# The last 512 tokens of a fused attention and MLP kernel, scored by four head groups of 128 tokens in place of one head group of 512

## The chip, the cores and the metric

The kernel runs on one core of one Trainium2 chip. The metric is the device time of one execution in microseconds (us); the median of three runs is given, and one more execution was profiled. A core has five engines that run side by side and wait for each other by semaphores: PE (TensorE: matrix products; PEld is its weight load), DVE (VectorE), ACT (ScalarE: activation functions such as exp), POOL (GpSimd) and SP (SyncE, which here issues the DMAs).

## What is computed

A transformer block with parallel branches over 2048 tokens of width 512: one layer norm, multi-query attention (32 heads of 16, one shared K and V), and an MLP of width 1792 with gelu.

```python
xn = _layernorm(x)                                  # (1, 2048, 512)
q = (xn @ wq).reshape(B, S, 32, 16)...              # 32 heads of 16
k, v = xn @ wk, xn @ wv                             # one K and V for all heads
p = softmax(einsum("bhqd,bkd->bhqk", q, k) * 0.25)  # no mask
attn = einsum("bhqk,bkd->bhqd", p, v)... @ wo
h = gelu(einsum("bsd,df->bsf", xn, w1) + b1)        # F = 1792
out = x + attn + einsum("bsf,fd->bsd", h, w2) + b2
```

All inputs and the output are bf16.

## The kernel before, in words

**Tiles.** The tokens are cut into 4 blocks of 512 (`TBW`; `NTB` = 4), the heads into 8 groups of 4 (`NGR`, `HG`), the keys into 16 tiles of 128. A score tile is 128 keys x 512 columns: one head of a group against the 512 tokens of a block. 4 blocks x 8 groups x 16 key tiles x 4 heads are 2048 tiles (`NTILE`), and a block and group pair, `gg` from 0 to 31, is a run of 64 of them (`TPG`). Three tiles make a unit; there are 683 units, numbered by `u`.

**Scores** (`scores`, L962). A unit's three scores are one trio on PE, in 32-row tiling, into half of the six score banks of PSUM; the two halves alternate. The weights are K, the moving operand is `QT[32 rows, g, :]`, 512 columns of group g.

**Exponentials.** Each tile takes one of two ways, as the table `DTAB` says with one letter per unit. Most go through ACT (`exp`, L983, the instruction at L999), two or three tiles per instruction, and then take one product with V. The others go through DVE: an affine step to int16 bits (`p1`, L1030), then in batches (`close_batch`) integer steps that make three more buffers (L1077) and a last step per tile (L1073), which POOL takes when it fits; each buffer and its shifted version are a weighted summand of the exponential, so such a tile needs five products with V (`pv_mm`, L1043).

**Product with V.** The products run in 32-column tiling: four of them, one per head of the group, stand side by side in PE and add into one bank, `pO`. V has a column of ones in row 16 of each head, so the denominators come with the sum.

**Normalization** (`o_evac`, L1087). When the 64 tiles of a group are through, DVE copies `pO` to `Of` (L1089). DMAs bring the denominators into `den` and the four heads' rows into `OfP`; for every second group DVE takes the reciprocals, they go to DRAM and come back spread over rows as `rbP`, and two multiplications of 128x256 (L1120, POOL or DVE) write `oTp` for the pair. Group 30 is normalized alone, with a half filled pair whose other rows carry b2 (`wopE`, L1112). The last group, 31, has a way of its own (`o_norm_last`): DVE copies (L1127), PE spreads the denominators with `selB` (L668), ACT takes the logarithm and exp(-ln) (L1134, L1137), and DVE multiplies (L1140).

**Side work.** Everything else PE does in the loop also runs in 32-column tiling through one bank, 7 (`mm4`, L674, four matmuls of 128*32 by 512, one set): Q for the next block (`q_pack`, and `q_m`, which writes an extra row per head into QT), the MLP's first product (`h_mm`), and the output tiles of 128 tokens x 512: the MLP's second product (`y_mm`, 14 sets), the attention's output product (`wo_mm`, 4 sets) and b2. Gelus run on ACT in two blocks, after units 182 and 512.

**The end.** In blocks 0 to 2 an output tile is closed by one DVE addition (`out_tile`, L1246) and a store. In block 3 a head group covers all 512 tokens, so no tile can be closed before the last group. `y_tile` (L1251) puts what it can into bank 7, with the first two of the four pairs (`FIN_G` = 2), and DVE sets three tiles aside in f32 (L1256); the fourth stays in bank 7. After the loop the last pairs' products go into the score banks 2, 3, 4 and bank 7, the last group's product (`wol`, 4 sets, one per tile) follows, DVE adds three tiles (L1362), ACT copies the fourth (L1365), and four stores follow.

**What sets the order.** A planner in the program (`Prog.schedule`, L230) lists all instructions with costs in us and picks for each engine the next one, simulating the engines with constants; the order it finds is fixed and written out per engine, with semaphore waits (`emit`). For PE it holds that each of the four column groups is busy for 0.216 per product, that four follow each other by 0.006, that the next round starts when all four are free, and that a change between score trios (rows) and the rest (columns) costs `SWITCH` = 0.1. Side work becomes due at units given by the tables `HP` (h_mm), `YP` (output tiles), `YF`, `QK` and `Q3` (Q). The chip doesn't see these numbers; only the order that comes out of them.

Of the kernel before, what the change touches and what calls it, by code (L numbers as in the profile page):

```python
# [10 lines left out]
P = 128  # L11
# [10 lines left out]
SWITCH = 0.1  # L22
WIN = 3.413
# [28 lines left out]
FIN_G = 2  # L52
FIN_F = 0
# [3 lines left out]
TBL = 1  # L57
DMASK = {".": (), "0": (0,), "2": (2,), "a": (0, 1), "b": (1, 2), "x": (0, 1, 2),
         "o": (0,), "t": (2,), "A": (0, 1), "B": (1, 2), "X": (0, 1, 2)}
CLOSE = "otABX"  # L60
DTAB = "ooo0tt.020t.0t.00o000.o0.0tt0..oo2222o.02.t02t02..o2o.22ot202.0.0oo.200t22.o0o22o0.0020.22t0.t.2o.t.o2ttto.00o2oo0..o2000o0ot.t.002o0002tt.200.o0to.o.t2otott0.t.2.0o000oo...000o2000toxXxB2to222t0020t.0t.oo202t.t.00t2o202ot02.0t0t.02.2oot2.o0t.00o2200220.o.2oo022.tot.ot02o002.2.t0tt02t2t...000ot..o222tt22t..202o.22.o0..002o.2o2tt0t.2t0.020t0..22t2o..02o2020t22.t0002t22o..o00t2.t.o2o20o2t02.0t2.0t.00t.2t2ott2ot0t2to.22.oto2..o200tt2t.0t002ot00..0too22o20tt2...02.ott.2t0.0ott..00t0.00oto..tt2t0202tot0t.0220toaBXXBto2o02.t202o0.02t.22ooo2t.2002o0.o00.o2ot.t202ooto.00o222t0..to200t0oo.2.0o.2t00o20o2t22.0t.tt0t2o2.0t.oo00t00o2.o.o02ot2.t.2ttt200oot.202o0.0t..totoo0.t2o2o.2.t2to..."
# [14 lines left out]
HP = ((87.13167,22,66.82083,147.91108,40.38849,110.84753,55.66665,14,50.53259,112,20.66845,152.08006,61.80125,39.6289),(150.38812,79.48637,93.96663,107.61124,166.80472,0,0,0,0,0,0,0,0,0),(291.76004,310.12719,295.27265,322.59733,262,325.24506,298.5666,286,298,435.55883,304,280,433.01683,498.53492),(475.57156,486,469.88268,498,442,0,0,0,0,0,0,0,0,0))  # L76
YP = ((201.09452,184.17265,220,250),(346.3059,388.90013,354.32695,420.90269),(522.38115,516.36879,560.84805,588.7863),(613.17749,604.45936,628.95944,659.10039))
# [37 lines left out]
class Prog:  # L115
# [84 lines left out]
    def pick_pe(self, t, cand, allr, mode, visit, cgbusy):  # L200
# [3 lines left out]
        if mode == "col":  # L204
            end = max(cgbusy)
            if t < end - 0.01:
                if t < end - 0.216 + 0.03:
# [22 lines left out]
    def schedule(self):  # L230
# [31 lines left out]
        opened = None  # L262
        aend = 0.0
# [9 lines left out]
        while left:  # L273
# [13 lines left out]
            if e == "pe":  # L287
                op = self.pick_pe(t, cand, ready["pe"], mode, visit, cgbusy)
                st = max([free["pe"]] + cgbusy) if mode == "col" else max([free["pe"], pend + SWITCH] + cgbusy)
# [97 lines left out]
            if e == "pe":  # L387
# [3 lines left out]
                if op.kind in ("pv", "side"):  # L391
                    cg = op.tag[1]
                    st = max(t, cgbusy[cg], free["pe"])
                    if mode != "col":
                        st = max([t, pend + SWITCH] + [c + SWITCH for c in cgbusy])
                    op.start = st
                    cgbusy[cg] = st + 0.216 * slow
# [15 lines left out]
                elif op.kind != "side":  # L413
                    m = {"S": "row", "side": "col"}.get(op.kind, "full")
                    w = SWITCH if m != mode else 0.0
# [13 lines left out]
            if e == "pe":  # L429
# [5 lines left out]
                pend = op.start + op.occ * slow  # L435
# [31 lines left out]
    def settle(self):  # L467
        free = {e: 0.0 for e, _ in self.SECTIONS}
        mode, cg, pend, aend = None, [0.0] * 4, 0.0, 0.0
        for op in self.ops:  # L470
# [3 lines left out]
            if op.eng == "pe":  # L474
                if op.kind in ("pv", "side") or (op.kind == "fill" and occ > 0.15):
                    t = max(t, cg[op.tag[1]]) if mode == "col" else max([t, pend + SWITCH] + [c + SWITCH for c in cg])
                    cg[op.tag[1]] = t + 0.216
                    mode, end = "col", t + 0.006
                else:
                    m = "row" if op.kind == "S" else "full"  # L480
                    w = SWITCH if m != mode else 0.0
                    t = max([t, pend + w] + [c + w for c in cg])
                    mode, end = m, t + occ
                pend = t + occ
# [8 lines left out]
    def emit(self):  # L493
# [4 lines left out]
        for op in self.ops:  # L498
# [40 lines left out]
def bass_parallel_sum__grouped_kv_mqa__dense_activation_gelu__prompt_kernel(  # L539
# [33 lines left out]
    with ExitStack() as es:  # L573
# [16 lines left out]
        wol = sb([P, D], bf, "wol")  # L590
# [14 lines left out]
        wopE = sb([P, D], bf, "wopE")  # L605
# [33 lines left out]
        oT = sb([P, TBW], bf, "oT")  # L639

# [287 lines left out]
        setup(lambda e: e.memset(wol[:], 0.0), w=["wol"], occ=0.4, due=24.0, after=late)  # L928
        setup(lambda e: e.tensor_copy(selB[:].rearrange("p (j r) -> p j r", j=4), ident[:, 16:113:32].unsqueeze(2).to_broadcast([P, 4, 32])),
              r=["ident"], w=["selB"], occ=0.3, due=24.0, after=late)  # L930
        setup(lambda e: e.memset(wopE[:], 0.0), w=["wopE"], occ=0.4, due=24.0, after=late)
        dma("sp", wop[:], A_wo.rearrange("(g p) n -> p g n", p=P), "d_wo", w=["wop"], after=late)
        dma("sp", wopE[0:64, :], A_wo[(H - 2 * HG) * Dh:(H - HG) * Dh, :], "d_we", w=["wopE"])
        dma("sp", wopE[64:65, :], B_b2.rearrange("(o n) -> o n", o=1), "d_we", w=["wopE"])
        for j in range(HG):
            dma("sp", wol[32 * j:32 * j + Dh, :], A_wo[(H - HG + j) * Dh:(H - HG + j + 1) * Dh, :], "d_wl", w=["wol"])
# [5 lines left out]
        TPG = HG * NT  # L942
        NTILE = NTB * NGR * TPG
# [17 lines left out]

        def scores(u):  # L962
# [3 lines left out]
            for i, t in enumerate(ts):  # L966
                gg, kt, j = tile_of(t)
                tb, g = divmod(gg, NGR)
# [3 lines left out]
                r += [k for k in q_rows(g) if k not in r]  # L972
# [113 lines left out]

        def o_evac(gg):  # L1087
            i = gg % 2
# [4 lines left out]
            end = gg == NTB * NGR - 2  # L1093
# [5 lines left out]
            if h or end:  # L1099
# [11 lines left out]
            if end:  # L1111
                dve(lambda e: e.memset(oTp[64:P, sl, :], 1.0), r=[("Of", i)], w=[("oTp", sl)], n=200, lock=True)  # L1112
            if h or end:
                n = 64 if end else P
# [107 lines left out]
        def wo_mm(tb, i, ps, start=False, bk=7, al=1.5, stop=False):  # L1222
            for n, p in enumerate(ps):
                pp = tb * NGR // 2 + p
                hs = [h for h in range(2) if 2 * pp + h < NTB * NGR - 1]
                assert all(2 * pp + h in onorm for h in hs) and 2 * (pp + NPR) + 1 not in onorm
# [184 lines left out]
```

## Time and profile before

| What | Value |
|---|---|
| median of three runs | 745.96 us (745.7 to 746.35) |
| the profiled execution, its own time | 746.57 us |
| its span in the profile | 744.8 us |
| exponentials on ACT (L999) | 678 instructions, 676.3 us |
| first step of DVE tiles (L1030) | 554 instructions, 375.0 us |
| matmuls of scores (L976) | 2048, mean 385 ns |
| last steps of DVE tiles: POOL, DVE (L1073) | 453 and 115 |

The span runs from the first to the last instruction of the profiled execution. Busy times of an engine are the union of its instructions' times; instructions overlap a little, so a mean duration is longer than the distance from one start to the next. An idle time is followed by what ended it.

### The profile page before, as it was taken

Reading aid. Unit: us, or ns where it says so; the run is one execution under the profiler, and the core shown is the slowest. Engines: PE = TensorE matmul, PEld = TensorE weight load, DVE = VectorE, ACT = ScalarE, POOL = GpSimd, SP = SyncE. Lnnn points to the kernel's source line nnn. Section 1 sums busy time; section 2 is a strip of 40 time slices with the busy share of each in tenths; the row PEclk is TensorE's granted clock in tenths of the full one; section 3 lists DMA queues with packets and bytes.
Section 4 is the critical chain, followed back from the end, with each engine's and each line's share of the span. In section 5 each row is a group of like instructions: output and inputs, shape, how many; then the busy total and the mean of one; then the engine's idle time right before and its main releaser. Section 6 shows DMA issues by size and latency. Waiting matters only on the chain.

```text
span 744.8 us, 22104 instructions
## 1 busy us (share of the span) xinstructions
PE 731.4 (98%) x9128; PEld 226.7 (30%) x9130; DVE 731.0 (98%) x1401; ACT 728.9 (98%) x759; POOL 389.3 (52%) x539
## 2 busy tenths in 40 slices
PE   7999999999999999999999999999999999999998
PEld 5332222222233222223222322223233323222223
DVE  7899999999999999999999999999999999999996
ACT  8899999999999999999999999999999999999996
POOL 5554565646314656553544655555634665556452
PEclk9999999999999999999999999999999999999999
DMA  9200100100010010100101110110001001010011
GB/s 310 70 16 20 31 9 16 26 8 18 12 36 18 14 46 24 24 24 11 36 5 30 32 31 22 22 27 14 23 14 28 20 16 45 16 39 17 13 39 33
DMA packets 32159, 23.41 MB, mean 31 GB/s; under 512 B 16386, under 2 KB 27580, under 8 KB 32060
## 3 DMA queue, kind: packets, MB, share of 16 engines
q1 hardware_dynamic: 31004, 21.97, 11.1%
q8 instruction: 73, 1.20, 0.7%
q14 instruction: 26, 0.21, 0.1%
q10 hardware_dynamic: 1056, 0.03, 0.1%
HBM read 13.15 MB, written 2.35 MB: 21 GB/s over the span
## 4 chain that ended last, share of the span: by engine, by line
ACT 65%; PE 30%; DVE 3%; DMA 1%; issue 0%; SPq 0%; POOL 0%
ACT E L999 64%; PE pAll L1043 13%; PE pAll L976 9%; PE pAll L674 7%; DVE Dt L1030 1%; DVE Dt L1077 1%; DMA x_sb<-in_A_x_dram 1%; PE pAll L668 0%; PE pAll L814 0%; DVE stats L763 0%; ACT xnT L819 0%; PE pAll L1372 0%; ACT ub L796 0%; DVE Dt L1073 0%; DVE QT L865 0%
## 5 line engine op out<-in xcount | busy, mean ns | idle before, releaser
L999 ACT ACTIVATE E<-pAll 128x1024 bf16<-128x1024 f32 (+1 forms) x678 | 676.3, 1212 | 3.0 <-PE pAll L976 2.7
L1073 POOL TENSOR_SCALAR Dt<-Dt 128x512 int16<-128x512 int16 x453 | 348.5, 769 | 318.8 <-DVE Dt L1077 143.6
L1043 PE MATMUL pAll<-Dt,V 128*32 128x512 bf16 x2840 | 414.3, 383 | 0.8 <-DVE Of L1089 0.8
L1030 DVE TENSOR_SCALAR Dt<-pAll 128x512 int16<-128x512 f32 (+1 forms) x554 | 375.0, 694 | 1.2 <-PE pAll L976 0.6
L1077 DVE TENSOR_SCALAR Dt<-Dt 128x1024 int16<-128x1024 int16 (+5 forms) x524 | 292.6, 582 | 0.3
L1043 PE MATMUL pAll<-E,V 128*32 128x512 bf16 x1480 | 278.4, 384 | 0.0
L976 PE MATMUL pAll<-QT,KT 32*128 32x512 bf16 x2048 | 267.4, 385 | 3.6 <-ACT E L999 1.4
L976 PEld LDWEIGHTS pAll<-QT,KT 32*128 32x128 bf16 x2048 | 66.8, 91 | 282.2 <-ACT E L999 265.2
L1043 PEld LDWEIGHTS pAll<-Dt,V 128*32 128x32 bf16 x2840 | 108.0, 95 | 110.5 <-issue 70.4
L674 PE MATMUL pAll<-xnT,w_sb 128*32 128x512 bf16 x896 | 104.7, 382 | 0.0
L1043 PEld LDWEIGHTS pAll<-E,V 128*32 128x32 bf16 x1480 | 66.3, 94 | 49.7 <-issue 36.0
L674 PE MATMUL pAll<-w_sb,x_sb 128*32 128x512 bf16 x448 | 71.7, 383 | 0.0
L674 PE MATMUL pAll<-w_sb,ub 128*32 128x512 bf16 x448 | 70.1, 383 | 0.0
L674 PE MATMUL pAll<-wop,oTp 128*32 128x512 bf16 x240 | 45.3, 383 | 0.0
L674 PEld LDWEIGHTS pAll<-xnT,w_sb 128*32 128x32 bf16 x896 | 29.8, 95 | 19.8 <-issue 8.8
L1073 DVE TENSOR_SCALAR Dt<-Dt 128x512 int16<-128x512 int16 x115 | 30.1, 281 | 0.0
L1120 POOL TENSOR_TENSOR oTp<-OfP,rbP 128x256 bf16<-128x256 f32 x29 | 23.2, 808 | 11.7 <-DVE Dt L1030 5.1
L674 PE MATMUL pAll<-xnT,wq_sb 128*32 128x512 bf16 x256 | 23.4, 383 | 0.0
L1089 DVE COPY Of<-pAll 128x512 f32<-128x512 f32 x31 | 21.0, 679 | 0.0
L1176 DVE TENSOR_SCALAR ub<-pAll,b1T 128x512 bf16<-128x512 f32 x28 | 20.8, 742 | 0.2 <-PE pAll L1043 0.2
L674 PEld LDWEIGHTS pAll<-w_sb,x_sb 128*32 128x32 bf16 x448 | 17.6, 95 | 8.1 <-issue 6.6
L674 PEld LDWEIGHTS pAll<-w_sb,ub 128*32 128x32 bf16 x448 | 17.6, 94 | 6.9 <-issue 5.7
(125 smaller groups left out, 256.4 us busy)
## 6 DMA issues: line engine op xcount, KB each, us to landing
OfP<-Of SPq DMA_DIRECT2D x124, 32.0 KB, 2.0
rbP<-rden_rows SPq DMA_DIRECT2D x124, 32.0 KB, 1.8
w_sb<-in_B_w_dram SPq DMA_DIRECT2D x2, 1792.0 KB, 13.4
x_sb<-in_A_x_dram SPq DMA_DIRECT2D x8, 256.0 KB, 4.6
x_sb<-in_A_x_dram SPq DMA_DIRECT2D x16, 128.0 KB, 2.3
QT<-qp SPq DMA_DIRECT2D x124, 16.0 KB, 1.8
out_dram<-x_sb SPq DMA_DIRECT2D x12, 128.0 KB, 1.8
wq_sb<-in_A_wq_dram SPq DMA_DIRECT2D x1, 512.0 KB, 6.5
```

Of the source, the lines that this page charges most:

```text
L674: add("pe", lambda e, c=c, j=j: e.matmul(o[c, :], l[:, c], rh, start=start, stop=stop, tile_position=(0, 32 * j)), r, [(k, j) for k in w] ...
L976: ins = e.matmul(o, l, rh, start=True, stop=True, tile_position=(q0, 0))
L999: o = act(lambda e: e.activation(E[:, s0:s0 + na, :], bank(b0, na).rearrange("p (a n) -> p a n", a=na), ACT.Exp, scale=LN2 / 128.0), w=[B( ...
L1030: op = dve(lambda e: e.tensor_scalar(Dt[:, s:s + n, :], bank(bk, n).rearrange("p (a n) -> p a n", a=n), float(127 * 128) + SPL_D, SPL_MIN, ...
L1043: add("pe", lambda e, a, b: e.matmul(pO[32 * j:32 * j + 32, :], V1[:, v, kt, :], rhs, start=a, stop=b, tile_position=(0, 32 * j)), r=r + [ ...
L1073: add("pool", lambda e, d=d, k=k: e.tensor_scalar(d, d, 1.0, float(k), ALU.mult, ALU.add), [], [(("D", base[o > 0] + q), o)], occ=PL_OCC, ...
L1077: dve(lambda e, d=view(o, nb), q=view(i, nb), k=k: e.tensor_scalar(d, q, float(k), None, ALU.add), r=keys(i), w=keys(o), n=nb * n * TBW, m ...
L1089: dve(lambda e: e.tensor_copy(Of[:, i, :], pO), w=["O", ("Of", i)], allow=0.0)
L1120: "pool", lambda e, c=c: e.tensor_tensor(oTp[0:n, sl, c], OfP[0:n, s, c], rbP[0:n, s, c], ALU.mult),
L1176: dve(lambda e: e.tensor_scalar(ubs[tb % 2][:, ft, :], pM, b1T[:, ft:ft + 1], None, ALU.add), r=["b1T"], w=M4 + [ukey(tb, ft)], n=TBW + 57 ...
```

## The change

In the last block a `gg` no longer stands for one group against 512 tokens but for four groups (0 to 3, then 4 to 7) against 128 tokens. The 64 tiles of a `gg` are still 16 key tiles x 4 heads, and a tile still has 512 columns, now 4 groups x 128 tokens. After each second `gg` 128 tokens have all their heads. So:

- `o_quarter` takes the place of `o_evac` for `gg` 24 to 30. It normalizes each `gg` by itself: one reciprocal, 8 DMAs into `OfP`, 8 into `rbP`, one multiplication of 128x256 into `oTq`, which lies in a part of `xnT` that is no longer needed.
- The first three output tiles of the block are closed by `out_tile` like those of the blocks ahead. The fourth (`y_last`) waits in bank 7 with the MLP, x and two of its four pairs; after the loop come four sets with the last `gg` (one per group, weights `wol`), one ACT copy and one store.
- `wol` is loaded at unit 300 into another part of `xnT` (`w_last`, 9 DMAs), with b2 in it; the memsets and loads of the old `wol` and `wopE` at the start go.
- The planner's constants change: 0.216 becomes `C_OCC` = 0.197 for the time that a column group is held, with 0.0105 more in the first round of a visit; 0.1 becomes 0.115 and 0.1055 for the changes to rows and to columns.
- The tables `DTAB`, `HP` and `YP` are others, from a search. `Q3`, `QK` and the gelu places stay.
- In `emit` a wait may name a later value of a semaphore that another wait of the same instruction implies already.

```diff
+SW_ROW = 0.115
+SW_COL = 0.1055
+C_OCC = 0.197
+C_FIRST = 0.0105
...
-YP = (...,(613.17749,604.45936,628.95944,659.10039))
+YP = (...,(593.39845,625,654.09462,657.83105))
...
-                        st = max([t, pend + SWITCH] + [c + SWITCH for c in cgbusy])
+                        st = r1 = max([t, pend + SW_COL] + [c + SW_COL for c in cgbusy])
                     op.start = st
-                    cgbusy[cg] = st + 0.216 * slow
+                    cgbusy[cg] = st + (C_OCC + (C_FIRST if st < r1 + 0.1 else 0.0)) * slow
...
-                t = max(t, best.pop(s, 0))
+                t = max(t, best.pop(s, 0), kn[s])
...
+        wol = xnT[:, :, TBW:2 * TBW]
+        oTq = xnT[:, :, 2 * TBW:3 * TBW]
...
+        def groups(gg):
+            if gg < G3:
+                return slice(gg % NGR, gg % NGR + 1), slice(0, TBW)
+            c = gg - G3
+            return slice(HG * (c % 2), HG * (c % 2) + HG), slice(P * (c // 2), P * (c // 2) + P)
...
-                pieces.append((bank(3 * x + i), KT[q0:q0 + 32, kt * P:(kt + 1) * P], QT[q0:q0 + 32, g, :], q0))
+                pieces.append((bank(3 * x + i).rearrange("p (a n) -> p a n", a=n), KT[q0:q0 + 32, kt * P:(kt + 1) * P],
+                               QT[q0:q0 + 32, gs, cs], q0))
...
+        def o_quarter(gg):
+            i = s = gg % 2
+            q, k = divmod(gg - G3, 2)
+            dve(lambda e: e.tensor_copy(Of[:, i, :], pO), w=["O", ("Of", i)], allow=0.0)
...
+            for h in range(2):
+                for j in range(HG):
+                    r0 = 64 * h + Dh * j
+                    dma("sp", OfP[r0:r0 + Dh, s, 0:2 * P].rearrange("p (a n) -> p a n", a=2),
+                        Of[32 * j:32 * j + Dh, i, :].rearrange("p (a h n) -> p h a n", a=2, h=2)[:, h], f"d_of{s}{h}",
+                        r=[("Of", i)], w=[("OfP", s, h, j)])
+            dve(lambda e: e.reciprocal(den[:, s, 0:1, :], den[:, s, 0:1, :]), r=[("den", s, 0)], w=[("den", s, 0)], n=136)
...
+            o = add("pool", lambda e: e.tensor_tensor(oTq[:, 2 * k:2 * k + 2, P * q:P * q + P], v3(OfP), v3(rbP), ALU.mult),
+                    keys, [("oTq", k, q)] + (tr(8, 12) if q == 0 else []), occ=ON_OCC, lat=PL_LAT, allow=PL_DUE, kind="pl", lock=True,
+                    docc=vcost(TBW // 2))
...
+        at(300, w_last)
...
-                    at(YP[tb][i], lambda tb=tb, i=i: y_tile(tb, i), 0.6)
-                at(YF, lambda tb=tb: wo_mm(tb, 3, range(FIN_G, NGR // 2), al=WF_ALLOW))
+                    at(YP[tb][i], lambda tb=tb, i=i: (out_tile if i < 3 else y_last)(tb, i), 0.6)
+                at(YF, lambda tb=tb: wo_mm(tb, 3, range(2), al=WF_ALLOW))
...
-        FB = (2, 3, 4, 7)
-        for i in range(3):
-            wo_mm(tb, i, range(FIN_G, NGR // 2), start=True, bk=FB[i], al=WF_ALLOW)
-        for i in range(4):
-            mm4(bank(FB[i]), oT[:, i * P:(i + 1) * P], wol[:, :], False, True,
-               r=[("oTl", i // 2), "wol"], w=[B(FB[i])], due=0.0)
...
+        for g in range(4):
+            mm4(pM, oT[:, g * P:(g + 1) * P], wol[:, g, :], False, g == 3, r=[("oTl", g // 2)] + WOL,
+                w=[B(7)], due=0.0)
+        dst, key = ub[:, 9, :], ("u", 0, 9)
+        act(lambda e: e.activation(dst, pM, ACT.Copy), w=M4 + [B(7), key])
+        store(tb, 3, dst, key)
```

More of the change, by code (lines that the diff above doesn't have):

```diff
@@ L262, in schedule @@
         opened = None
+        r1 = 0.0
         aend = 0.0
@@ L967, in scores @@
                 gg, kt, j = tile_of(t)
-                tb, g = divmod(gg, NGR)
+                gs, cs = groups(gg)
                 q0 = 32 * j
-                pieces.append((bank(3 * x + i), KT[q0:q0 + 32, kt * P:(kt + 1) * P], QT[q0:q0 + 32, g, :], q0))
+                n = gs.stop - gs.start
+                pieces.append((bank(3 * x + i).rearrange("p (a n) -> p a n", a=n), KT[q0:q0 + 32, kt * P:(kt + 1) * P],
+                               QT[q0:q0 + 32, gs, cs], q0))
                 r.append(("KT", kt))
-                r += [k for k in q_rows(g) if k not in r]
+                r += [k for g in range(gs.start, gs.stop) for k in q_rows(g) if k not in r]
             def fn(e):
```

107 lines of the change are left out of this document (58 added, 49 removed).

## The prediction

> **What bounds the kernel now.** I read the page's busy shares and its chain of waits first, then the busy time by stretches, then the costliest groups by shape, and last the timeline of the final 20 us.
>
> ```profile
> span 744.8 us, 22104 instructions
> ...
> PE 731.4 (98%) x9128; PEld 226.7 (30%) x9130; DVE 731.0 (98%) x1401; ACT 728.9 (98%) x759; POOL 389.3 (52%) x539
> ```
>
> ```profile
> ACT 65%; PE 30%; DVE 3%; DMA 1%; issue 0%; SPq 0%; POOL 0%
> ```
>
> Three engines are busy for 98% of the span, and the chain runs 65% through ACT. So no single engine can be relieved at the price of another: a change gains where all three wait at once, that is at the two ends, or by better order in between. The stretches of the loop say how much the order has left (columns: length, then busy us and count of PE, PEld, DVE, ACT, POOL):
>
> ```profile
> 100.00:190.00 90.00, 89.24 (x1053) 25.98 (x1057) 89.83 (x171) 90.00 (x90) 50.31 (x66) 1.00 0.07 17
> 190.00:280.00 90.00, 89.98 (x1200) 28.69 (x1188) 89.97 (x165) 88.69 (x88) 38.48 (x51) 1.00 0.10 25
> ```
>
> and the sum of all eight from 30 to 725 us:
>
> ```profile
> sum 695.00, PE 691.44 PEld 206.91 DVE 693.71 ACT 691.80 POOL 366.91; mean PE 86.43 PEld 25.86 DVE 86.71 ACT 86.47 POOL 45.86
> ```
>
> From 30 to 725 us ACT lacks 695.00 - 691.80 = 3.2 us and DVE 1.3 us. In the best stretch ACT lacks nothing, in the worst 1.31 us of 90. The granted clock is 1.00 throughout, so the clock plays no part. The end is where all three idle:
>
> ```profile
> 724.53 11.13 ACT L999 ACTIVATE E<-pAll 128x1536 bf16<-128x1536 f32 x10
> ```
>
> The last exponentials end at 724.53 + 11.13 = 735.66, and the span ends at 744.8: 9.1 us without score work. That stretch is what the change is about.
>
> **The change: the end.** The timeline of DVE alone after the last score, then two cuts of the whole timeline:
>
> ```profile
> 736.27 0.89 DVE L1127 COPY Of<-pAll 128x256 f32<-128x256 f32 x2 [1.43 <-PE pAll L1043]
> 738.73 0.76 DVE L1140 TENSOR_TENSOR oT<-Of,rbP 128x256 bf16<-128x256 f32 x2 [1.57 <-ACT rbP L1137]
> 739.74 1.89 DVE L1362 TENSOR_TENSOR ub<-pAll,ub 128x512 bf16<-128x512 f32 x3 [0.25 <-PE pAll L674]
> ```
>
> ```profile
> 739.21 0.83 PE L674 MATMUL pAll<-wol,oT 128*32 128x512 bf16 x12
> 739.54 0.10 PEld L674 LDWEIGHTS pAll<-wol,oT 128*32 128x32 bf16 x4 [0.21 <-DVE oT L1140]
> ```
>
> ```profile
> 741.16 0.39 PE L674 MATMUL pAll<-wol,oT 128*32 128x512 bf16 x3
> 741.64 0.60 ACT L1365 ACTIVATE ub<-pAll 128x512 bf16<-128x512 f32 x1 [2.64 <-PE pAll L674]
> ```
>
> The chain of waits over the same time, and the last store:
>
> ```profile
> 736.82 1.09 PE pAll L668 x4
> 737.91 3.71 PE pAll L674 x62
> ```
>
> ```profile
> 742.59 0.45 SPq L681 DMA_DIRECT2D out_dram<-ub  x1
> ```
>
> The normalization of the last head group (copy, sum row spread by PE, logarithm and exponential on ACT, product) has its second half ready at 739.54, when the weights of the last product can be loaded. But PE is not free: after the spreading matmuls it has 62 side matmuls in one piece (3.71 us), most of them output products of all four tiles. The last of them starts at 741.16 and ends at 741.55; ACT copies the fourth tile until 742.24; its store is issued only at 742.59, since SP is still at the stores of the tiles ahead.
>
> The change leaves one tile there. Its last product is four rounds (one per head group) of four matmuls. A round of four takes 0.22 us, as three steps between wide rounds show, and a score trio can start 0.32 us after the last one:
>
> ```profile
> 583.33 0.39 PE L1043 MATMUL pAll<-E,V 128*32 128x512 bf16 x2
> ...
> 583.99 0.39 PE L1043 MATMUL pAll<-Dt,V 128*32 128x512 bf16 x4
> 584.31 0.39 PE L976 MATMUL pAll<-QT,KT 32*128 32x512 bf16 x3
> ```
>
> Rounds 1 and 2 need only the first half and start at 739.21 and 739.43; 3 and 4 at 739.65 and 739.87. The last ends at 740.26, ACT starts 0.09 later as now, at 740.35, and ends at 740.95 in place of 742.24: 1.29 us. The store has no other ahead of it and is issued at about 741.0 in place of 742.59: **1.6 us earlier**. The three DVE additions of L1362 leave the path with it; three like them come earlier instead, where three additions of L1256 (the same shape) leave, so DVE's loop work keeps its size.
>
> This holds if PE has done nearly all other work by then. The side matmuls in the last two stretches:
>
> ```profile
> 704.80:736.20 31.40, 14.35 (x113) 4.16 (x117) 1.00 0.11 28
> 736.20:745.00 8.80, 4.32 (x74) 1.64 (x66) 0.99 0.19 61
> ```
>
> Before has 74 left at 736.20, of which 44 had to wait (three tiles' third and fourth output products in score banks, and the last product). After, the third tile is due at unit 654 and the fourth at 658, about 704.8 us (a unit is three score tiles). They hold 19 and 17 sets of four (14 of the feed-forward and 4 output products and the bias, or 14 with the residual and 2), 144 matmuls. At the present pace 113 of them are done by 736.20, so 31 stay. With 16 of the last product that is 47, 12 rounds of 0.22 = 2.6 us, and 1.09 for the spreading: 3.7 us after 736.2, or 739.9, inside the 740.26 of the chain. Six more matmuls would fill the gap. I take **-1.5 us**, between -1.6 (chain alone) and -0.3 (74 left as now; only the store's wait goes).
>
> **The change: the loop.** The table of the search moves single tiles between ACT and DVE. Counted in the two tables: 569 tiles on the DVE path in place of 568, 547 exponentials of two tiles and 127 of three in place of 546 and 128, and 257 DVE batches in place of 262.
>
> ```profile
> L999 ACT ACTIVATE E<-pAll 128x1024 bf16<-128x1024 f32 x546 | 524.5, 1136 | 2.0 <-PE pAll L976 1.7
> L999 ACT ACTIVATE E<-pAll 128x1536 bf16<-128x1536 f32 x128 | 193.4, 1554 | 1.0 <-PE pAll L976 1.0
> ```
>
> ```profile
> L1030 DVE TENSOR_SCALAR Dt<-pAll 128x512 int16<-128x512 f32 x545 | 361.7, 680 | 1.1 <-PE pAll L976 0.6
> L1077 DVE TENSOR_SCALAR Dt<-Dt 128x1024 int16<-128x1024 int16 x174 | 70.7, 416 | 0.2
> ...
> L1077 DVE TENSOR_SCALAR Dt<-Dt 128x512 int16<-128x512 int16 x106 | 29.0, 281 | 0.1
> ```
>
> ```profile
> PEld pAll L976 <- ACT E L999: 265.2, 636, 0.8
> ```
>
> ACT: 1554 - 1136 = 0.42 us less: **-0.4 us**. DVE: one tile more is 0.68 and three slots of 0.135 (416 - 281), so +1.1; five batches fewer are ten instructions fewer, each with 0.146 that does not depend on size (281 - 135), so -1.5; one memset of the old last pair also goes. DVE stays about level, -0.4 or lower, and takes nothing from ACT's gain. PE gets four matmuls more for the tile and one output set more (21 against 20): two rounds, 0.4 us; 636 of its score trios wait for ACT, 265.2 us in all, and that wait hides it. Without the cover it is 0.4.
>
> What the new order does to the waits can't be counted. Bounds from the stretches: all like the best, -3.2 us; all like the worst, 1.31 x 695 / 90 = 10.1 in place of 3.2, so +6.9. The nearest row is before's own total, no change. I go a fifth of the 3.2 below it, **-0.6**, for one reason: the planner's old numbers make a round of four 0.216 + 3 x 0.006 = 0.234 us, the new ones 0.197 + 0.018 = 0.215, and the trace has 0.22, so the new order was laid out on nearer times.
>
> [...]
>
> Costs that I set at nothing: two memsets on POOL (52% busy) and six loads go from the prologue; nine loads of the last weights come at unit 300, hundreds of us ahead of use. POOL gets seven products of 128x256 for the last eight groups in place of eight. SP gets 18 issues for each of seven groups, 126 in place of 67: at 0.6 each some 35 us more, in a queue that waits 182.5 us for one line of DVE alone. The score trios of the last 512 tokens read their moving operand in four pieces of 128 columns. The trace has no such read, but one that is not a plain row either (a broadcast of stride zero):
>
> ```profile
> SPq L681 <- DVE Dt L1030: 182.5, 26, 20.2
> ```
>
> ```profile
> L674 PE MATMUL pAll<-ident,b1row 128*32 128x512 bf16 x72 | 6.8, 383 | 0.0
> ```
>
> At 383 ns it takes what the plain ones take (0.38 to 0.39), so 0, or 0.006 x 171 trios = 1 us on either side.
>
> **Sum.** -1.5 - 0.4 - 0.6 = -2.5. The profiled execution took 746.57 for a span of 744.8; after it would be 744.1 with a span of 742.3. The median of the runs before is 745.96, 0.6 below that execution, so 743.5 for the median.
>
> **Rivals.**
>
> *PE's backlog stays (744.7).* The third tile drifts past the loop, so that more than one tile is still open at the end and the change doesn't do what it says. For it: before's third tile was meant for unit 629 and PE still had 30 avoidable matmuls left. Against it: 31 + 16 fit. Then the tail gives 0.3 only: 745.96 - 0.3 - 0.4 - 0.6.
>
> *The last quarter's first half comes late (745.5).* Each group is now normalized by itself, with 18 DMAs in place of 19 for a pair.
>
> ```profile
> 718.91 0.60 SPq L681 DMA_DIRECT2D den<-Of  x1
> 719.55 2.42 SPq L681 DMA_DIRECT2D OfP<-Of  x4
> ...
> 724.47 1.71 SPq L681 DMA_DIRECT2D rbP<-rden_rows  x4
> ```
>
> ```profile
> rbP<-rden_rows SPq DMA_DIRECT2D x124, 32.0 KB, 1.8
> ```
>
> Eight OfP copies from 719.55 at 0.6 end at 724.4; the reciprocals' store and its landing take about 2.2, 726.6; eight rbP at 0.43 end at 730.0 and land at 731.8; with the product it is 732.7. PE wants it by 737.9; its queue, the last product too, stands behind that wait. It costs only from a delay of 5 us on: 2 us, so 745.5, if the delay is 7. [...]
>
> *The second half of the last Q comes late (745.7).* Group 25 now reads heads' groups 4 to 7, which were needed first at group 28. Their last rows:
>
> ```profile
> 578.79 2.52 SPq L681 DMA_DIRECT2D QT<-mT  x4
> ```
>
> ```profile
> 0.00:584.40 584.40, 208.80 (x1602) 52.31 (x1602) 1.00 0.12 33
> ```
>
> They are issued until 581.31 and land 1.8 us later (the landing of the copies above), 583.1. Group 25 begins with score 1600, in the trio at 584.31, the last of 1602 in this window. The margin is 1.2 us. On SP the eight rbP copies of the previous pair are next to them; ahead of them they would cost 8 x 0.43 = 3.4, so a trio 2.2 us late with all of PE behind it, and ACT and DVE waiting for its scores: 743.5 + 2.2.
>
> *The new order starves ACT (slower, 749).* Place: the score trios of the loop. With the shorter round the planner puts more rounds ahead of a trio. Where rounds are not filled by four and still take 0.22, each visit is longer than planned, the trio late, and ACT waits. Price: if every stretch becomes like 190 to 280, +6.9, so 751; at two thirds of it 749. It decides from 747.45 on, where the loop loses 3.4 us against now: 3.4 / 678 = 5 ns per exponential. For it: ACT's 98% is a delicate balance, and a table is only as good as its model. Against it: the best stretches show that the order can hold ACT at 100% for 90 us.
>
> **Chances.** Forecast 0.62; backlog 0.13, late Q 0.07, late quarter 0.03, starved ACT 0.15. A measurement of this kernel tells 0.2%, 1.5 us, from no change: faster is below 744.47, slower above 747.45. Half of the backlog case falls on the faster side: faster 0.68, same 0.17, slower 0.15. The range goes from all idle of the loop gone (745.96 - 1.6 - 0.4 - 3.2 = 740.8, put at 740.5) to 746.6, beyond the first three rivals; the starved ACT is left out.
>
> **What would show it.** The tail: one ACT copy and one store behind the last product, ACT's copy 4.1 us after the accumulator's copy starts (before 5.4), no side matmuls of the third tile behind it. The loop: exponentials 547 and 127, ACT's lack from 30 to 725 near 2.6. Wrong if the last product waits for PE, if a trio near 584 waits for a DMA, or if ACT's lack exceeds 6 us.

## The result

The kernel after takes 743.98 us (median of 10 runs, 743.81 to 745.04) against 746.06 (10 runs, 745.7 to 746.35): a ratio of 0.9974, 95% interval 0.9964 to 0.9983. That is 2.1 us faster. The forecast was 743.5 in a range of 740.5 to 746.6.

The profiled execution took 743.81 us. The head of its page, and the shares of its chain of waits:

```profile
span 742.1 us, 22084 instructions
...
PE 729.0 (98%) x9117; PEld 229.8 (31%) x9117; DVE 727.0 (98%) x1374; ACT 728.4 (98%) x759; POOL 407.1 (55%) x554
```

```profile
ACT 58%; PE 36%; DVE 5%; DMA 0%; issue 0%; SPq 0%
```

Three engines are still busy for 98% of the span: nothing was relieved, and the gain must lie where all three wait. The stretches of the loop that were shown of before, the last two that serve as yardstick further down, and the sum of all eight from 30 to 725 us:

```profile
100.00:190.00 90.00, 89.53 (x1042) 26.46 (x1034) 89.84 (x163) 90.00 (x91) 56.50 (x71) 1.00 0.09 17
190.00:280.00 90.00, 89.97 (x1223) 29.55 (x1222) 89.65 (x164) 88.89 (x88) 47.57 (x60) 1.00 0.11 26
...
370.00:460.00 90.00, 89.75 (x1153) 27.25 (x1150) 89.76 (x170) 90.00 (x91) 49.51 (x64) 1.00 0.10 25
460.00:550.00 90.00, 88.89 (x1071) 26.32 (x1067) 89.54 (x167) 89.33 (x91) 50.86 (x69) 1.00 0.08 19
...
sum 695.00, PE 691.55 PEld 212.05 DVE 692.98 ACT 692.01 POOL 386.14; mean PE 86.44 PEld 26.51 DVE 86.62 ACT 86.50 POOL 48.27
```

ACT (the fourth busy time) lacks 695.00 - 692.01 = 3.0 us here, 3.2 before. So the loop hardly changed; now the end, in the timelines of ACT, DVE and SP:

```profile
732.93 1.53 ACT L1009 ACTIVATE E<-pAll 128x1536 bf16<-128x1536 f32 x1
```

```profile
735.01 0.88 DVE L1169 COPY Of<-pAll 128x256 f32<-128x256 f32 x2 [2.35 <-PE pAll L1053]
735.81 0.41 DVE L1122 TENSOR_TENSOR xnT<-OfP,rbP 128x256 bf16<-128x256 f32 x1
737.65 0.76 DVE L1182 TENSOR_TENSOR oT<-Of,rbP 128x256 bf16<-128x256 f32 x2 [1.43 <-ACT rbP L1179]
```

```profile
739.31 0.60 ACT L1407 ACTIVATE ub<-pAll 128x512 bf16<-128x512 f32 x1 [1.38 <-PE pAll L681]
```

```profile
718.28 5.43 SPq L688 DMA_DIRECT2D OfP<-Of  x8
...
725.45 3.60 SPq L688 DMA_DIRECT2D rbP<-rden_rows  x8
...
739.93 0.36 SPq L688 DMA_DIRECT2D out_dram<-ub  x1
```

The last exponential ends at 734.47. One copy of ACT and one store are left, as planned; the store is issued 0.02 us after the copy ends, where the one of before waited 0.35 behind three others. I cut both profiled executions into the same pieces. The loop runs from the start of the second exponential to the end of the last one (the first exponential lies alone, before the loop is under way):

| Piece, us | before | after | difference |
|---|---|---|---|
| start of the first exponential | 24.69 | 24.10 | -0.59 |
| loop | 709.42 | 708.82 | -0.60 |
| last exponential to DVE's copy of the accumulator | 0.61 | 0.55 | -0.06 |
| from there to ACT's copy of the fourth tile | 5.37 | 4.30 | -1.07 |
| from there to the end of the span | 3.19 | 2.76 | -0.43 |
| the three end pieces together | 9.17 | 7.61 | -1.56 |

End and loop make -2.16, and the medians differ by 2.08. The start makes 0.59 more in this pair alone; the first exponential of the runs below starts between 24.03 and 24.69 in kernels with the new layout and between 24.32 and 24.69 in kernels with the old one, so I don't count it.

### The profile page after: what moved, and what is told of

The parts are those of the page before. It is cut to its first block, busy times and chain, and to the rows that moved or that the text cites. A ratio compares the mean times of both kernels' runs of the same rounds, so it can differ in the third digit from the quotient of the medians.

```text
span 742.1 us, 22084 instructions
## 1 busy us (share of the span) xinstructions
PE 729.0 (98%) x9117; PEld 229.8 (31%) x9117; DVE 727.0 (98%) x1374; ACT 728.4 (98%) x759; POOL 407.1 (55%) x554
## 4 chain that ended last, share of the span: by engine, by line
ACT 58%; PE 36%; DVE 5%; DMA 0%; issue 0%; SPq 0%
ACT E L1009 58%; PE pAll L1053 17%; PE pAll L986 11%; PE pAll L681 7%; DVE Dt L1040 1%; DVE Dt L1087 1%; DVE stats L770 1%; PE pAll L675 1%; DMA x_sb<-in_A_x_dram 0%; PE pAll L1414 0%; DVE ub L806 0%; ACT xnT L826 0%; DVE Dt L1083 0%; ACT ub L803 0%; DVE mv L784 0%
## 5 line engine op out<-in xcount | busy, mean ns | idle before, releaser
L1083 POOL TENSOR_SCALAR Dt<-Dt 128x512 int16<-128x512 int16 x470 | 367.2, 781 | 301.5 <-DVE Dt L1087 130.3
L1053 PE MATMUL pAll<-Dt,V 128*32 128x512 bf16 x2845 | 430.5, 383 | 1.0 <-DVE Of L1134 0.8
L1040 DVE TENSOR_SCALAR Dt<-pAll 128x512 int16<-128x512 f32 x555 | 376.5, 694 | 2.3 <-PE pAll L986 1.1
L1087 DVE TENSOR_SCALAR Dt<-Dt 128x1024 int16<-128x1024 int16 (+8 forms) x514 | 292.4, 592 | 0.2
L1053 PE MATMUL pAll<-E,V 128*32 128x512 bf16 x1479 | 282.9, 385 | 0.0
L1053 PEld LDWEIGHTS pAll<-Dt,V 128*32 128x32 bf16 x2845 | 115.1, 94 | 120.9 <-issue 78.4
L681 PE MATMUL pAll<-xnT,w_sb 128*32 128x512 bf16 x896 | 117.8, 382 | 0.0
L1053 PEld LDWEIGHTS pAll<-E,V 128*32 128x32 bf16 x1479 | 66.2, 94 | 44.0 <-issue 31.0
L681 PE MATMUL pAll<-w_sb,x_sb 128*32 128x512 bf16 x448 | 73.6, 381 | 0.0
L681 PE MATMUL pAll<-w_sb,ub 128*32 128x512 bf16 x448 | 72.6, 382 | 0.0
L681 PEld LDWEIGHTS pAll<-xnT,w_sb 128*32 128x32 bf16 x896 | 33.5, 95 | 21.8 <-issue 9.8
L681 PE MATMUL pAll<-wop,oTp 128*32 128x512 bf16 x192 | 34.7, 384 | 0.0
L1083 DVE TENSOR_SCALAR Dt<-Dt 128x512 int16<-128x512 int16 x99 | 25.5, 282 | 0.0
L1162 POOL TENSOR_TENSOR oTp<-OfP,rbP 128x256 bf16<-128x256 f32 x23 | 18.5, 814 | 7.6 <-DVE Dt L1087 4.4
L681 PE MATMUL pAll<-xnT,wq_sb 128*32 128x512 bf16 x256 | 21.1, 383 | 0.5 <-DVE ub L1218 0.5
L681 PEld LDWEIGHTS pAll<-w_sb,x_sb 128*32 128x32 bf16 x448 | 19.8, 95 | 4.0 <-issue 1.4
L681 PEld LDWEIGHTS pAll<-w_sb,ub 128*32 128x32 bf16 x448 | 19.2, 95 | 4.1 <-issue 2.3
L681 PE MATMUL pAll<-b2row,ones 128*32 128x512 bf16 x60 | 17.6, 383 | 0.0
```

The lines of the kernel that those rows point to most:

```text
L681: add("pe", lambda e, c=c, j=j: e.matmul(o[c, :], l[:, c], rh, start=start, stop=stop, tile_position=(0, 32 * j)), r, [(k, j) for k in w] ...
L1040: op = dve(lambda e: e.tensor_scalar(Dt[:, s:s + n, :], bank(bk, n).rearrange("p (a n) -> p a n", a=n), float(127 * 128) + SPL_D, SPL_MIN, ...
L1053: add("pe", lambda e, a, b: e.matmul(pO[32 * j:32 * j + 32, :], V1[:, v, kt, :], rhs, start=a, stop=b, tile_position=(0, 32 * j)), r=r + [ ...
L1083: add("pool", lambda e, d=d, k=k: e.tensor_scalar(d, d, 1.0, float(k), ALU.mult, ALU.add), [], [(("D", base[o > 0] + q), o)], occ=PL_OCC, ...
L1087: dve(lambda e, d=view(o, nb), q=view(i, nb), k=k: e.tensor_scalar(d, q, float(k), None, ALU.add), r=keys(i), w=keys(o), n=nb * n * TBW, m ...
L1162: "pool", lambda e, c=c: e.tensor_tensor(oTp[0:n, sl, c], OfP[0:n, s, c], rbP[0:n, s, c], ALU.mult),
```

## Experiments

### Structure or tables: four kernels that told something else

**Theory A**: the layout shortens the end by itself, whatever constants and tables stand in the planner; the loop is worth some us more or less. **Rival B**: the layout alone brings little, and the new constants and the searched tables make the gain. Four kernels mix the parts. The first is the kernel after with all of the planner's old numbers, the second the kernel before with all of the new ones, the third after with old tables alone, the fourth after with old constants alone:

```diff
 # e1 (from after): constants and tables of before; e3: the tables alone; e4: the constants alone
-SW_ROW = 0.115
-SW_COL = 0.1055
-C_OCC = 0.197
-C_FIRST = 0.0105
+SW_ROW = SW_COL = 0.1
+C_OCC = 0.216
+C_FIRST = 0.0
...
-DTAB = "..."   HP = ...   YP[0:3] = ...
+DTAB, HP and YP[0:3] of before
 # e2 (from before): the constants, DTAB, HP and YP[0:3] of after
```

> The new layout of the last block with the planner's old constants and the old DTAB, HP and first three rows of YP (the last row of YP is the new one, which the layout needs). Theory A, the layout shortens the end by itself: from the end of the last exponential to the end of the span 7.5 to 8.2 us (before 9.2, after 7.6), whatever the tables; the loop, from the second exponential's start to the last one's end, 709 to 711 us, since the table was not made for this layout; 744.5 to 746. Theory B, the gain came from the search and the planner's constants, the layout only moves work: the end may be shorter but the loop gives it back, 746 or more.

> The old layout and the old end with the new constants, the new DTAB, HP and first three rows of YP (last row of YP the old one). Theory A: the end stays at 9.2 us, the loop at 709 to 710; 745.4 to 746.5. Theory B: most of the gain is here, 744 to 744.5.

> After with the old DTAB, HP and first three rows of YP; constants and layout are the new ones. Theory A: the end 7.5 to 8.2 us, the loop longer by 0.5 to 3 us than after's 708.8, since the table was laid out on other constants; 744.5 to 747. Theory B: like before or slower, 746 to 748, and the end takes no part in it.

> After with the planner's old constants (0.1, 0.1, 0.216 and 0); tables and layout are the new ones. Theory A: the end 7.5 to 8.5 us (the planner thinks PE slower, so more side work may stay behind), the loop longer by 0.5 to 3 us; 744.5 to 747. Theory B: if the constants carry the gain it is gone here, 746 or more; if the table does, 744.

| Kernel | median, us | ratio to before (95%) | loop | end |
|---|---|---|---|---|
| e1: after, old constants and tables | 785.37 | 1.0537 (1.0508 to 1.0566) | 744.3 | 13.2 |
| e2: before, new constants and tables | 774.05 | 1.0373 (1.0356 to 1.0390) | 741.2 | 9.3 |
| e3: after, old tables | 767.11 | 1.0281 (1.0266 to 1.0297) | 729.5 | 10.1 |
| e4: after, old constants | 788.21 | 1.0570 (1.0554 to 1.0586) | 750.3 | 9.8 |

The ratios, here and below, hold a kernel against runs of before made beside it; their medians were 746.09 here, 745.82 for e5 to e8 and 745.61 for e9 and e10.

Both theories missed by 20 to 40 us, nearly all of it in the loop. The waits of ACT in e1 (line waited for: us in total, times, longest) show how:

```profile
ACT E L1009 <- PE pAll L1053: 23.7, 13, 6.7
...
ACT ub L1407 <- PE pAll L681: 7.2, 1, 7.2
```

In the kernel after, this view has no such row: no exponential of ACT waits for a product with V (L1053). Here 13 do: a buffer of exponentials isn't free, because PE has not yet come to the products that read it. And POOL takes fewer last steps of DVE tiles; the rest fall to DVE. Whether that is a cause of the drift or follows from it isn't shown. The groups by shape of after, then of e1:

```profile
L1083 POOL TENSOR_SCALAR Dt<-Dt 128x512 int16<-128x512 int16 x470 | 367.2, 781 | 301.5 <-DVE Dt L1087 130.3 <-PE pAll L1053 60.8 <-DVE Dt L1040 40.8
...
L1083 DVE TENSOR_SCALAR Dt<-Dt 128x512 int16<-128x512 int16 x99 | 25.5, 282 | 0.0
```

```profile
L1083 POOL TENSOR_SCALAR Dt<-Dt 128x512 int16<-128x512 int16 x367 | 273.4, 745 | 415.8 <-DVE Dt L1087 171.8 <-PE pAll L1053 87.9 <-DVE Dt L1083 64.4
```

The end does not hold either: in e1 ACT's last copy waits 7.2 us for PE, as the second row of its waits says. This is the backlog of the forecast's first rival, in a plan that drifted. So e1 to e4 can't tell what layout, constants or tables are worth. Each of them changes the planner's first choices, and every choice after them comes out another way. At most a smaller part of their loss goes with the granted clock, whose mean is 0.96 to 0.98 in one to three stretches of each of these four loops (last section).

### Does a table fit any other order?

**Theory C**, formed on that: a searched table fits the one order that it was searched with, and no other, however close the numbers. **Rival D**: the four kernels lost their time to numbers that are really worse; a nudge of 0.1 ns costs nothing.

```diff
 # e7 (from after)
-C_FIRST = 0.0105
+C_FIRST = 0.0106
 # e9 (from before)
-SWITCH = 0.1
+SWITCH = 0.1001
 # e10 (from after): DTAB's letter of unit 400, some 440 us into the run
-t
+2
```

> After with one constant of the planner moved by a tenth of a nanosecond: C_FIRST 0.0106 in place of 0.0105. Theory C, from the first four runs: the tables hold for one planned order alone, and any nudge near the start rolls all of it anew, so the loss of e1 to e4 was neither the layout's nor the constants': 755 to 775, POOL taking fewer than 420 of the 569 last steps (after 470). Rival, the tables are good for this layout and these constants in general: 743.5 to 746, POOL's count near 470.

> The kernel before with one constant of the plan a ten-thousandth of a microsecond larger (0.1 to 0.1001 us for a change of operand side), from the first instruction on. Theory C (a searched table holds for one planned order alone, the old one as much as the new): 765 to 785 us, the loop 730 to 750 us where it was 709.4, POOL takes fewer than 420 of the last steps (before 453), and the end after the last exp keeps the three tiles' work, 8.5 to 10 us. Rival D (the nudge hurts only the new tables, because they were fitted more closely): 744 to 750 us, the loop within 2 us of 709.4, POOL near 450.

> The kernel after with one letter of the filler table changed at unit 400 of 700, some 440 us into the run, and nothing before it. Theory C: the stretches up to 430 us are those of after within 0.1 us of ACT's busy time, and only those behind it lose; about a third of the 22 us that the nudge at the start cost is the most, so 747 to 752 us, with ACT's lack from 460 to 725 us above 3 us. Rival D (one letter is one step's worth, and the rest of the tables still fits): 743.5 to 745 us, the loop within 1 us of 708.8.

| Kernel | median, us | ratio to before (95%) | loop | end | last steps on POOL |
|---|---|---|---|---|---|
| e7: after, one constant 0.1 ns larger | 766.04 | 1.0271 (1.0252 to 1.0289) | 730.2 | 8.6 | 404 |
| e9: before, one constant 0.1 ns larger | 775.04 | 1.0395 (1.0365 to 1.0425) | 737.3 | 10.1 | 377 |
| e10: after, one letter | 749.27 | 1.0048 (1.0026 to 1.0071) | 712.2 | 9.5 | 448 |

Theory C holds for both tables: a tenth of a nanosecond costs the new one 21 us of loop and the old one 28. What costs ACT most in e9 is the wait that costs it most in e1:

```profile
ACT E L999 <- PE pAll L1043: 22.2, 11, 3.6
```

e10 shows it inside one run. Its stretches, to be held against those of after above:

```profile
100.00:190.00 90.00, 89.53 (x1046) 26.49 (x1034) 89.84 (x163) 90.00 (x91) 56.42 (x71) 1.00 0.08 17
...
370.00:460.00 90.00, 89.75 (x1151) 27.36 (x1148) 89.72 (x169) 90.00 (x91) 48.81 (x63) 1.00 0.10 25
460.00:550.00 90.00, 88.39 (x1049) 26.10 (x1045) 89.79 (x173) 87.86 (x89) 45.92 (x59) 0.98 0.08 19
```

Up to 460 us PE, DVE and ACT are busy as in after to 0.06 us. Behind the letter ACT lacks 2.14 in place of 0.67 in the very next stretch. The loop loses 3.4 us in all and the end 1.9, for one letter of 683. Rival D falls.

### Experiments that keep the order

So the end has to be tried without touching what is planned ahead of it. e5 gives the kernel after the end's work of before back: nine sets of four matmuls (two output products and one last product for each of three tiles), three DVE additions, and three stores ahead of the last one, to a spare tensor. e6 is the kernel before with only one tile at the end; the rows of its three other tiles are left unwritten. e8 leaves out of after the 14 matmuls of the fourth tile that PE still has behind the last product with V.

```diff
 # e5 (from after), behind the loop
+for i in range(3):
+    for p in (2, 3):
+        mm4(bank(2 + i), oTq[:, p, i * P:(i + 1) * P], wop[:, p, :], p == 2, False, ...)
+for i in range(3):
+    mm4(bank(2 + i), oT[:, i * P:(i + 1) * P], wol[:, i, :], False, True, ...)
...
+    dve(lambda e, i=i: e.tensor_tensor(ub[:, 6 + i, :], bank(2 + i), ub[:, i, :], ALU.add), ...)
+    dma("sp", extra[i * P:(i + 1) * P, :], ub[:, 6 + i, :], ...)
 # e6 (from before)
-        for i in range(3):
-            wo_mm(tb, i, range(FIN_G, NGR // 2), start=True, bk=FB[i], al=WF_ALLOW)
-        for i in range(4):
+        for i in (3,):
             mm4(bank(FB[i]), oT[:, i * P:(i + 1) * P], wol[:, :], False, True, ...)
-        for i in (0, 1, 3, 2):
+        for i in (3,):
 # e8 (from after), behind the planning
+        late = {id(o) for o in pr.ops[end + 1:]} & {id(o) for o in ylast}
+        pr.ops = [o for o in pr.ops if id(o) not in late]
```

> After with the work of the old end put behind the loop once more: nine more sets of four matmuls into banks 2, 3 and 4 (two output products and one last product for each of three tiles), three DVE additions and three stores, to a spare tensor, so that the kernel's own output is untouched. Tables, constants and layout are after's, and the planned order is after's until the last 3 us of the loop. Theory A, the three tiles are what the end of before cost: nine rounds at 0.216 are 1.9 us of PE, ACT's last copy 5.7 to 6.3 us after the accumulator's copy starts (after 4.3), the end 9.2 to 9.8 us (after 7.6, before 9.2), 745.5 to 746.1 in all. Rival, the end is hidden behind the normalization anyway and the gain was the loop's: end below 8.0, 744.0 to 744.3.

> Before with the end of three tiles left out: their nine sets of matmuls behind the loop, their three DVE additions and stores. Those three tiles' rows of the output are not written. The planned order is before's until the last microsecond of the loop. Theory A: PE has 38 of 74 matmuls left, the chain of the normalization sets the end, ACT's copy 4.1 to 4.4 us after the accumulator's copy (before 5.4), the end 7.5 to 7.8 us (before 9.2), 744.4 to 744.7. Rival, hidden anyway: end above 8.8, 745.8 to 746.1.

> After with 14 matmuls of the fourth tile's feed-forward product left out, those that the plan puts behind the last product with V (the last 128 tokens' rows are wrong by that). The order of the rest is after's. If PE's leftover holds up the chain at all, as 4.3 against the 4.1 us of the prediction suggests, ACT's copy comes 0.1 to 0.3 us earlier: 4.0 to 4.2, the end 7.3 to 7.5 us, 743.7 to 743.9 in all. If the chain alone sets it: unchanged, 4.3. If PE's leftover sets all of it: 0.8 us earlier (3.5 rounds of 0.216), 3.5.

| Kernel | median, us | ratio to before (95%) | loop | to DVE's copy | to ACT's copy | to the end |
|---|---|---|---|---|---|---|
| before | 746.06 | 1 | 709.42 | 0.61 | 5.37 | 3.19 |
| e6: before, one tile | 744.10 | 0.9976 (0.9968 to 0.9985) | 709.43 | 0.58 | 3.80 | 2.75 |
| after | 743.98 | 0.9974 (0.9964 to 0.9983) | 708.82 | 0.55 | 4.30 | 2.76 |
| e5: after, old end's work | 746.10 | 1.0005 (0.9996 to 1.0014) | 708.82 | 1.36 | 5.33 | 3.21 |
| e8: after, no leftover | 743.54 | 0.9969 (0.9958 to 0.9981) | 708.83 | 0.55 | 4.11 | 2.74 |

The loops of kernels with the same order repeat to 0.01 us, so each difference to the kernel that the edit started from lies in the end. **e5** is back at the time of before, but in part by coincidence. Its loop is still 0.60 shorter, and its end is 9.90, where before has 9.17 (expected: 9.2 to 9.8). Two of its three pieces are those of before to 0.04 us, so the work of three tiles accounts for the 1.5 us that after gained in these two. The first was not expected: DVE's copy comes 0.8 later, since the added output products stand in part ahead of the last product with V on PE. The 0.60 us of the loop is not what e5 tests. PE there, then the end of the chain, DVE's copy, and SP:

```profile
734.71 0.60 PE L681 MATMUL pAll<-wop,xnT 128*32 128x512 bf16 x8
...
735.36 0.38 PE L1053 MATMUL pAll<-Dt,V 128*32 128x512 bf16 x1
```

```profile
737.88 3.21 PE pAll L681 x42
741.11 0.60 ACT ub L1418
```

```profile
735.78 0.88 DVE L1169 COPY Of<-pAll 128x256 f32<-128x256 f32 x2 [2.82 <-PE pAll L1053]
```

```profile
740.53 1.52 SPq L688 DMA_DIRECT2D extra_rows<-ub  x3
742.10 0.43 SPq L688 DMA_DIRECT2D out_dram<-ub  x1
```

ACT's copy ends at 741.71, and the last store waits until 742.10, 0.39 us behind the three others: that is the third piece. **e6** says the same from the other side. Without three tiles the end of the old layout falls to 7.13 (expected: 7.5 to 7.8), 0.48 below that of after. Of this, 0.32 lies between DVE's product and ACT's copy (1.34 here, 1.66 in after), where its last product is one set and not four; 0.18 lies ahead of DVE's product (2.46 against 2.64), the place of the leftover that e8 measures. ACT and SP of e6:

```profile
739.93 0.60 ACT L1363 ACTIVATE ub<-pAll 128x512 bf16<-128x512 f32 x1 [1.07 <-PE pAll L674]
```

```profile
740.56 0.36 SPq L681 DMA_DIRECT2D out_dram<-ub  x1
```

**e8** asks what PE's leftover costs in after. DVE's copy and last product, PE's spreading between them, and ACT's copy:

```profile
735.12 0.88 DVE L1169 COPY Of<-pAll 128x256 f32<-128x256 f32 x2 [2.34 <-PE pAll L1053]
...
737.58 0.76 DVE L1182 TENSOR_TENSOR oT<-Of,rbP 128x256 bf16<-128x256 f32 x2 [1.24 <-ACT rbP L1179]
```

```profile
735.60 1.16 PE L675 MATMUL pAll<-Of,selB 128*128 128x256 f32 x4 [0.37 <-DVE Of L1169]
```

```profile
739.23 0.60 ACT L1411 ACTIVATE ub<-pAll 128x512 bf16<-128x512 f32 x1 [1.38 <-PE pAll L681]
```

Here PE idles ahead of the spreading and waits for the copy. The product starts 737.58 - 735.12 = 2.46 us behind the copy, in after 737.65 - 735.01 = 2.64; from the product to ACT's copy it is 1.65 here and 1.66 there. So the leftover costs 0.2 us, all of it ahead of the spreading, and what lies behind is hidden by the normalization. The end is 7.40 in place of 7.61, as expected (7.3 to 7.5); the median is 0.44 lower, but the intervals of the two ratios overlap. An emptier PE has no more than the 0.2 to give, and no version that beats after came out of these runs: e6 and e8 leave work out.

## Why the prediction was right, point by point

**The end, -1.5: measured -1.56.** The forecast's count was 31 side matmuls left and 16 of the last product. The side matmuls (L681) in two stretches (length, then PE's busy time and count), and the chain of waits behind the loop:

```profile
704.80:734.94 30.14, 16.21 (x125) 4.80 (x127) 1.00 0.13 34
734.94:743.00 8.06, 3.25 (x41) 1.05 (x35) 0.90 0.05 16
```

```profile
734.91 0.86 PE pAll L681 x10
735.78 1.06 PE pAll L675 x4
736.84 2.45 PE pAll L681 x31
```

At 734.94, the place that 736.20 was in before (0.07 us ahead of the accumulator's copy), 41 are left: 25 and the 16 of the last product, so PE was six ahead of the forecast. And the last product doesn't wait for PE: its 16 are the end of the chain's 31, the 15 ahead of them have all started by 737.86, and its first weight load waits for DVE's product:

```profile
738.13 0.12 PEld L681 LDWEIGHTS pAll<-xnT,oT 128*32 128x32 bf16 x8 [0.39 <-DVE oT L1182]
```

What the forecast had wrong is the place of the others. It took the time from the accumulator's copy to DVE's product as in before (2.46 us), but ten side matmuls stand ahead of the spreading in the chain, and it is 2.64. So ACT's copy comes 4.3 us after the accumulator's and not 4.1; e8, without 14 of them, has the 4.11. That the sum still came out is in part luck: ACT's copy was forecast 1.29 us earlier and came 1.13 earlier (0.06 + 1.07), and what follows it was forecast 0.3 us shorter and got 0.43 shorter.

**ACT's exponentials, -0.4.** The groups by shape are those counted in the table, 547 and 127:

```profile
L1009 ACT ACTIVATE E<-pAll 128x1024 bf16<-128x1024 f32 x547 | 524.9, 1110 | 2.2 <-PE pAll L986 2.0
...
L1009 ACT ACTIVATE E<-pAll 128x1536 bf16<-128x1536 f32 x127 | 192.0, 1536 | 0.5 <-PE pAll L986 0.5
```

1536 - 1110 = 0.43 us for one column block less; ACT's busy time on the page fell by 0.5, from 728.9 to 728.4. With the loop's -0.60 that leaves -0.18 for the waits.

**The waits of the loop, -0.6: measured -0.2.** This is the term that was mis-sized; ACT's lack went from 3.2 to 3.0, not to 2.6. The reason given for it, that an order laid out on nearer times waits less, is not supported: e4 changes just those constants, and its order drifts like any other. Whether the new constants are better with a table searched for them stays open; that would take a search of its own. With nothing for the waits the forecast would have been 743.5 + 0.6 = 744.1, and 743.98 lies nearer to that than to 743.5. What makes a trio's step longer than a round's isn't shown; in the chain of after it is 0.32 us behind a round, against 0.21 from round to round (before 0.32 and 0.22):

```profile
730.09 0.21 PE pAll L681 x4
730.31 0.01 PE pAll L1053
730.31 0.32 PE pAll L986 x3
```

**DVE about level: it fell by 4.0 us**, from 731.0 to 727.0, as POOL took 470 of the last steps and DVE 99, against 453 and 115. The count of tiles and batches could not show that, since the planner chooses who takes a last step. It moved no time: from 30 to 725 us ACT and PE are busy for 692.01 and 691.55 of the 695, before for 691.80 and 691.44.

**The reads in four pieces, 0.** They cost nothing. The mean over all 2048 is 384 ns where it was 385, and the 488 from 570 us on, all read in four pieces, took 384 to 386 ns:

```profile
L986 PE MATMUL pAll<-QT,KT 32*128 32x512 bf16 x2048 | 267.1, 384 | 2.8 <-ACT E L1009 1.6 <-DVE R L916 0.6 <-DVE Dt L1087 0.2
```

None of their 2.8 us of waiting is for a DMA. **Late Q** did not occur: SP has the last rows of Q ahead of the pair's eight copies, not behind them.

```profile
576.89 2.52 SPq L688 DMA_DIRECT2D QT<-mT  x4
579.45 3.68 SPq L688 DMA_DIRECT2D rbP<-rden_rows  x8
```

**Late last quarter** neither: its eight last copies are issued until 729.05 (forecast 730.0). But the forecast overlooked where its product stands. It gave the quarter 5 us of room (732.7 against 737.9); the product runs on DVE at 735.81, behind the accumulator's copy, and is done at 736.22, 0.2 us before ACT's logarithm, which overwrites `rbP`, starts at 736.44. In e8, with PE emptier, this product is what the logarithm waits for last:

```profile
736.38 0.85 ACT L1176 ACTIVATE rbP<-pAll 128x256 f32<-128x256 f32 x2 [1.81 <-DVE xnT L1122]
```

The forecast gave the copies of half the size the times of whole ones, as an estimate. The landing bears it out: half the bytes land only 0.1 us sooner, after 1.8 us in place of 1.9:

```profile
OfP<-Of SPq DMA_DIRECT2D x96, 32.0 KB, 1.9
...
OfP<-Of SPq DMA_DIRECT2D x56, 16.0 KB, 1.8
```

**A starved ACT** did not occur in the kernel after, but the forecast had its place and its price wrong. I priced an order that doesn't fit at 3.4 to 6.9 us, from the worst stretch of a kernel whose order had been searched. Orders that were not searched cost 21 to 42 us of loop (e1 to e4, e7, e9). The place was wrong too: in these six kernels ACT waits above all for PE's products with V to free its buffers (11.9 to 24.0 us), not for score trios. Such a row could not be had from the trace of before, where that wait doesn't occur.

## What to carry to other kernels

Here, with three engines busy at 98%, the gain that added up directly lay where all of them wait, at the end: the 1.56 of its 9.17 us that were won came within 0.1 us of what one timeline and one count of matmuls gave, with two small errors against each other, while the 4.0 us that DVE got less busy moved no time. A searched table belongs to one order: compare searched with searched, and test a part by an edit that leaves the order ahead of it as it is, or else the experiment measures the search. A worst stretch of a tuned loop is no bound for what an untuned one costs.

## What the runs showed that was not expected

- Loops with the same order repeat to 0.01 us (708.82, 708.82, 708.83; 709.42, 709.43), and 0.1 ns in a planner's constant moves the loop by 21 and 28 us.
- In e10 the granted clock fell. The mean clock of its three runs is 0.995 each, where after has 0.998 or 1.000. Its stretches about the place: the longest time without a matmul (PE busy 0.00 of 0.91), the 3.41 us ahead of the fall (PE busy 2.22), and the fall:

```profile
515.26:516.17 0.91, 0.00 (x2) 0.01 (x2) 0.91 (x3) 0.91 (x2) 0.00 (x0) 1.00 0.14 36
```

```profile
513.87:517.28 3.41, 2.22 (x18) 0.61 (x15) 3.41 (x8) 3.41 (x4) 0.00 (x0) 1.00 0.06 16
```

```profile
516.00:518.00 2.00, 1.63 (x15) 0.51 (x15) 2.00 (x5) 2.00 (x3) 0.00 (x0) 0.83 0.12 29
518.00:520.00 2.00, 2.00 (x23) 0.41 (x15) 2.00 (x3) 1.29 (x2) 1.34 (x1) 0.50 0.13 33
520.00:522.00 2.00, 2.00 (x35) 0.71 (x31) 2.00 (x5) 0.79 (x2) 0.79 (x2) 0.82 0.20 38
```

The clock is 0.50 in the middle, and the three stretches lose 0.34 + 1.00 + 0.36 = 1.7 us of full clock, as 3.4 us at half would. ACT lacks 0.71 + 1.21 in the last two, so a part of what the letter cost may be this. In the profiled executions of e1 to e4 the clock fell too. Its mean is 0.96 from 100 to 190 us and 0.98 from 370 to 460 in e1; 0.98, 0.98 and 0.96 in three stretches of e2 (190 to 280, 280 to 370, 460 to 550); 0.98 in two of e3 (280 to 370, 460 to 550) and in one of e4 (550 to 640). By the means over the whole span (0.989 of 783.3 us, 0.990 of 776.4, 0.993 of 765.4, 0.998 of 786.3) the four lack 8.6, 7.8, 5.4 and 1.6 us of full clock, and their loops lost 35, 32, 21 and 42 us; as an estimate, no more than the former went with the clock. In e7 and e9 the clock is 1.00 in every stretch from 30 to 725 us, and their loops lost 21 and 28 us without it.

How busy PE was doesn't decide alone: in before it was busy for 1.04 of the 3.41 us from 740.50 on, less than the 2.22 in e10, and the clock was still 1.00 in the 0.89 us up to the end of the span. What tells the two apart stays open.

```profile
740.50:743.91 3.41, 1.04 (x18) 0.32 (x10) 1.12 (x2) 0.60 (x1) 0.00 (x0) 1.00 0.45 149
743.91:744.80 0.89, 0.00 (x0) 0.00 (x0) 0.00 (x0) 0.00 (x0) 0.00 (x0) 1.00 0.06 17
```
